# A chunked attention with a Fourier mix and an MLP: last weighting beside the next batch's first scores, and normed tiles made sooner

## The chip, the cores and the metric

The kernel runs on one core of a Trainium2 chip. The metric is device time in microseconds, the median of several runs. A profile is one more execution, recorded by the hardware; its span runs from its first to its last instruction, and its own device time is somewhat longer than its span.

## The reference

For 8 batches, 8 heads, 576 positions and 64 values a head: attention within chunks of 64 positions, then a two-dimensional Fourier transform whose real part is added to the attention's output, then a normalisation and a two-layer MLP, all in fp32.

```python
scores = scale * q_c @ k_c.T            # per chunk of 64
attn = softmax(scores)                  # minus the row maximum, exp, over the row sum
x = attn @ v_c                          # (B, S, H*D) = (8, 576, 512)
u = x + real(fft(fft(x, axis=1), axis=2))
un = (u - mean(u)) / sqrt(var(u) + 1e-6)
out = u + maximum(un @ w_ch1, 0) @ w_ch2     # 512 -> 2048 -> 512
```

## The kernel before

**Tiles and groups.** A tile is 128 positions of a batch (two chunks). A batch has four: two "lo" tiles from its start and two "hi" tiles from its end, read backwards, since the transform is folded about the middle. The ninth chunks of two batches share a "rest" tile, so even batches count five tiles and odd ones four. The MLP works on nine groups of four tiles: one for each batch, and a last one with the four rest tiles.

**The MLP** runs group after group and is the main line of the program. Groups 0 (both layers) and 1 (first layer) are plain: `up_first`, `up_plain`, `down_plain`. After that each layer is a scheme with seven products of half-size blocks in place of eight: `up_halves` (L997) for the first layer, in four pairs of row blocks, and `down_halves` (L1042) for the second. Both count o = 0 to 6 for the product and r = 0, 1 for the half that it serves. Each product goes to a half of a PSUM tile, `pa` (o = 0, 1, 4) or `pb` (o = 2, 3, 5, 6), and is evicted before the next one is needed: in `up_halves` o = 0 and o = 4 by ScalarE (L1019, L1029), the others by VectorE (L1021, L1023, L1025, L1031, L1034), with ScalarE's Relu after them. `operands` (L916 to L920) makes sums of the layer's results on VectorE and GpSimd.

**The attention and transform of the next batch** are generators of small steps (`side`, `attention`, `fourier`) that the last loop of the program (L1188 on) mixes into the MLP: after each `yield` of the MLP it takes as many steps as are due by a linear rule. So a batch's attention falls partly into a down phase and partly into the next up phase, and its transform into the down phase after that. For each tile `att_T` turns q and k (VectorE, and an extra column by GpSimd for lo tiles, L350), `att_S` makes the scores (16 matmuls of 64x64, L380), `softmax` takes the maximum and subtracts it on VectorE (L393, L395), `exponential` is ScalarE's, `att_P` transposes, and `att_V` weights v (16 matmuls of 64x65, L428) and divides on VectorE (L441 to L445). Within a batch the scores of tile n + 1 stand right behind the weighting of tile n. The first scores of a batch are a step of their own (L583, L584), which comes due in a down phase. After hi tiles `fold` (L487) makes sums and differences on GpSimd.

**From transform to MLP.** `fourier` ends with `mixed`, `both`, `added` and `means` (L686 to L720): for each pair of tiles a matmul group, VectorE's and GpSimd's additions, VectorE's statistics (L632, L633) and ScalarE's rstd (L636, L637). Then `normed` (L806) makes a normalised tile `un` on VectorE (L824), and `turned` (L827) transposes it on TensorE (L329) and copies it to `unT`, by ScalarE for even tiles and by VectorE for odd ones (L837, L835). `combined` (L839) forms differences of the turned tiles. `down_halves` calls these for the next group between its own products; it counts k = 2*o + r.

**PSUM buffers.** `ps_t`, two buffers, serves transposes, the mix, two of the transform's products and the weighting, which takes both. `ps_a`, one buffer, serves the scores and the transform's other products. `ps_f`, four buffers, is the MLP's.

**The start.** The first batch's attention and transform run ahead of everything (`attention_early`, `fourier_early`). `keep_warm` (L1139) issues matmuls on zeros into a spare tile, so that TensorE has something to do in the gaps.

Each engine works through its own instructions in the order of the program text as executed; waits are semaphores.

Of the kernel before, what the change touches and what calls it, by code (L numbers as in the profile page):

```python
# [16 lines left out]
def kernel(  # L17
# [33 lines left out]
    B, H, S, D = q.shape  # L51
# [321 lines left out]
    def att_S(n):  # L373
        a, b = qT.pop(n), kT.pop(n)
        sc = ps_a.tile([128, 2, 512], FP32, tag="att", name="sc")
        for j in range(NJ):
            for e in range(2):
                for c in range(2):
                    r0, t0 = e * D, c * CH
                    nc.tensor.matmul(  # L380
                        out=sc[t0:t0 + CH, e, j * CH:(j + 1) * CH],
                        lhsT=a[r0:r0 + D, 2 * j + c, 0:CH],
                        rhs=b[r0:r0 + D, 2 * j + c, 0:CH],
                        start=True,
                        stop=True,
                    )
        scs[n] = sc
# [139 lines left out]
    def attention_early():  # L527

        lo, hi = first[0], first[1] - 1

        def ready(n):
            if n == at[LO, 0, 1]:
                shift_early(0)
            if n == at[HI, 0, 1]:
                fold(0, 1)
            if n == at[HI, 0, 0]:
                fold(0, 0)
            if n + 3 > hi:
                load_v(n + 3)

        att_T(lo)
        att_S(lo)
        for n in range(lo, hi + 1):
            if n < hi:
                att_T(n + 1)
            softmax(n)
            if n > lo:
                att_V(n - 1)
                ready(n - 1)
            if n < hi:  # L550
                att_S(n + 1)
            if n in (lo, hi):
                keep_warm(1)
            att_P(n)
        shift_early(1)
        fold(0, NM)
        keep_warm(1)
        att_V(hi)
        ready(hi)
        keep_warm(3)  # L560
        turn_tables()
        round_next()
        round_next(put_off)

    def attention(b):

        lo, hi = first[b], first[b + 1] - 1

        def ready(n):

            if n == at[LO, b, NM - 1]:
                shift(b)
            for i in range(NM):
                if n == at[HI, b, i]:
                    fold(b, i)
            if n == at[HI, b, 0]:
                fold(b, NM)
            return kind(n) == HI

        if b > 1:  # L580


            att_S(lo)  # L583
            softmax(lo)  # L584
            yield
            for n in range(lo, hi + 1):
                exponential(n)
                if n + 1 < NT:
                    att_T(n + 1, "q")
                yield  # L590
                att_P(n)
                if n + 1 < NT:
                    att_T(n + 1, "k")
                yield
                att_V(n)
                if n < hi:
                    att_S(n + 1)
                    softmax(n + 1)
                if n + 3 < NT:
                    load_v(n + 3)  # L600
                yield ready(n)
            return
        att_T(lo)
        yield
        for n in range(lo, hi + 1):
            att_S(n)
            softmax(n)
            yield
            if n + 1 < NT:
                att_T(n + 1)  # L610
            yield
            if n > lo:
                att_V(n - 1)
                if n + 2 < NT:
                    load_v(n + 2)
                yield ready(n - 1)
            att_P(n)
            yield
        att_V(hi)
        if hi + 3 < NT:  # L620
            load_v(hi + 3)
        yield ready(hi)
# [204 lines left out]
    def turned(g, s):  # L827
        if s >= len(groups[g]):
            return
        if s == 0:  # L830
            unTs[g] = one_p.tile([128, KD, G * 128], FP32, tag="unT", name="unT")
        unT, un = unTs[g], uns.pop((g, s))
        pt = turn(lambda j: un[:, j * 128:(j + 1) * 128])
        if s % 2 and g > 1:
            nc.vector.tensor_copy(unT[:, :, s * 128:(s + 1) * 128], pt)  # L835
        else:
            nc.scalar.copy(unT[:, :, s * 128:(s + 1) * 128], pt)  # L837
# [204 lines left out]
    def down_halves(g, h1):  # L1042
        pas, pbs = {}, {}
        for o in range(NO):
            w = slab2[((g - first_of[2]) * NO + o) % NS2]
            for r in range(2):
                cl, ch = slice(r * 128, (r + 1) * 128), slice(256 + r * 128, 256 + (r + 1) * 128)
                low, high = groups[g][r], groups[g][2 + r]
                olow, ohigh = os_[:, 2 * r], os_[:, 2 * r + 1]
                a, b = tmp[:, r, 0], tmp[:, r, 1]  # L1050
                if o == 0:
                    pas[r] = ps_f.tile([128, 2, 256], FP32, tag="ff", name="pa")
                if o == 2:
                    pbs[r] = ps_f.tile([128, 2, 256], FP32, tag="ff", name="pb")
                dst = (pas, pas, pbs, pbs, pas, pbs, pbs)[o][r][:, (0, 1, 0, 1, 0, 0, 1)[o]]
                lhs = (
                    h1[:, 0:HF, cl], ys[:, :, cl], xs[:, :, cl], h1[:, 0:HF, ch],
                    h1[:, HF:KF, cl], ys[:, :, cl], h1[:, HF:KF, ch],
                )[o]
                for m in range(HF):  # L1060
                    nc.tensor.matmul(  # L1061
                        out=dst, lhsT=lhs[:, m], rhs=w[:, m],
                        start=(o in (0, 2) and m == 0), stop=(m == HF - 1), skip_group_check=True,
                    )
                if o == 0:
                    nc.scalar.copy(a, dst)
                elif o == 1:
                    nc.vector.tensor_tensor(out=b, in0=dst, in1=a, op=ALU.add)
                elif o == 2:
                    nc.vector.tensor_tensor(out=a, in0=dst, in1=b, op=ALU.add)  # L1070
                elif o == 3:
                    nc.vector.tensor_tensor(out=ohigh[:, HM:DM], in0=dst, in1=ohigh[:, HM:DM], op=ALU.add)
                    nc.gpsimd.tensor_tensor(out=olow[:, HM:DM], in0=b, in1=natural(low)[:, HM:DM], op=ALU.add)
                    nc.gpsimd.tensor_tensor(out=ohigh[:, 0:HM], in0=b, in1=natural(high)[:, 0:HM], op=ALU.add)
                elif o == 4:
                    nc.vector.tensor_tensor(out=olow[:, 0:HM], in0=dst, in1=natural(low)[:, 0:HM], op=ALU.add)
                elif o == 5:
                    nc.vector.tensor_tensor(out=olow[:, HM:DM], in0=dst, in1=olow[:, HM:DM], op=ALU.add)
                    store(low, olow)
                else:  # L1080
                    nc.vector.tensor_tensor(out=ohigh[:, 0:HM], in0=dst, in1=ohigh[:, 0:HM], op=ALU.add)  # L1081
                    store(high, ohigh)
                k = 2 * o + r
                if g + 1 < NG:
                    for j in range(G):
                        if k == 4 + 2 * j:
                            normed(g + 1, j)
                        if k == 5 + 2 * j:
                            turned(g + 1, j)
                            if j >= 2:  # L1090
                                combined(g + 1, j - 2)
                if r == 1:
                    if o == 1:
                        for j in range(0, HF, 2):
                            two = ys[:, j:j + 2]
                            nc.gpsimd.tensor_tensor(
                                out=two, in0=h1[:, HF + j:HF + j + 2, lo], in1=two, op=ALU.subtract
                            )
                    if o == 2:
                        for i in range(2):  # L1100
                            nc.gpsimd.tensor_tensor(
                                out=os_[:, 2 * i + 1, HM:DM], in0=tmp[:, i, 0],
                                in1=natural(groups[g][2 + i])[:, HM:DM], op=ALU.add,
                            )
                    fetch(2)
                yield
# [7 lines left out]
    with tc.manual_schedule():  # L1114
# [24 lines left out]
        def keep_warm(times):  # L1139

            for _ in range(times):
                nc.tensor.matmul(out=idle[:, 0:NQ], lhsT=warm[:, 0:128], rhs=warm[:, 0:NQ], start=True, stop=True)
# [130 lines left out]
```

## Time and profile before

| | |
|---|---|
| runs | 1107.84, 1108.06, 1110.43 us; median 1108.06 |
| profiled execution | 1109.99 us, span 1108.2 us |
| TensorE matmul | 1079.4 us busy, 97% of the span |
| VectorE, ScalarE, GpSimd | 53%, 27%, 25% |
| DMA | 192.73 MB, mean 174 GB/s |
| granted TensorE clock, mean | 0.998 |

Each row of a timeline gives start, length, engine, line, operation, what it writes from what, sizes and count, and in brackets the engine's idle time before it with what ended it. Most matmuls leave two records, and the records of a back-to-back row overlap, so distances are best taken from start to start. A list of waits gives total, number and longest. A row of stretches gives the busy time of each engine with its instructions, then the clock granted to TensorE in parts of full speed, and the DMA's share and rate.

### The profile page before, as it was taken

How to read it: one execution, taken by the hardware profiler on the slowest of the kernel's cores; microseconds unless marked ns; L12 is line 12 of the kernel's file. 1: busy time of each engine (PE TensorE's matmuls, PEld its weight loads, DVE VectorE, ACT ScalarE, POOL GpSimd, SP SyncE). 2: the span in 40 equal slices, each digit the busy share in tenths (PEclk: the TensorE clock that was granted, in tenths of full speed). 3: DMA queues.
4: the chain of work that ended last, by engine and by line, in shares of the span. 5: the costliest groups of instructions: out<-in, count | busy, mean ns of one | idle time of the engine just before them, and what ended most of it. 6: DMA issues, size and time to landing. Idle time of an engine off the chain costs nothing. (4 is left out here: it accounts for less than half of the span.)

```text
span 1108.2 us, 18749 instructions
## 1 busy us (share of the span) xinstructions
PE 1079.4 (97%) x7010; PEld 849.1 (77%) x7010; DVE 582.1 (53%) x1260; ACT 297.5 (27%) x725; POOL 277.4 (25%) x403
## 2 busy tenths in 40 slices
PE   8899999999999999999999999999999999999998
PEld 6644454447887888888888888788888888888887
DVE  4798987325566365663556455625554434323521
ACT  4588453212112311322022212221133102201210
POOL 4200102354405140244024220424042401120130
PEclk9999999999999999999999999999999999999999
DMA  7767656679566546683559357753653355446232
GB/s 169 227 178 193 154 169 229 177 245 287 182 188 191 162 141 199 197 249 108 168 170 251 115 167 211 202 178 132 202 168 111 114 183 178 134 152 200 85 114 76
DMA packets 147970, 192.73 MB, mean 174 GB/s; under 512 B 66126, under 2 KB 104014, under 8 KB 140712
## 3 DMA queue, kind: packets, MB, share of 16 engines
q1 hardware_dynamic: 145620, 190.20, 56.8%
q8 instruction: 56, 0.92, 0.3%
q0 software_dynamic: 512, 0.68, 0.3%
q10 hardware_dynamic: 1748, 0.66, 0.2%
q14 instruction: 34, 0.28, 0.1%
HBM read 167.22 MB, written 24.12 MB: 173 GB/s over the span
## 5 line engine op out<-in xcount | busy, mean ns | idle before, releaser
L920 POOL TENSOR_TENSOR h<-h 128x256 f32<-128x256 f32 x64 | 56.0, 880 | 269.0 <-PE pb L1014 153.1
L1061 PE MATMUL pa<-wb,h 128*128 128x256 f32 x512 | 114.4, 380 | 0.0
L1061 PE MATMUL pb<-wb,h 128*128 128x256 f32 x512 | 114.2, 380 | 0.0
L1014 PE MATMUL pb<-unT,wa 128*128 128x256 f32 x448 | 107.0, 382 | 3.7 <-DVE wa L1023 3.4
L1014 PE MATMUL pb<-wa 128*128 128x256 f32 x448 | 107.2, 382 | 2.6 <-DVE h L1031 2.6
L1061 PEld LDWEIGHTS pa<-wb,h 128*128 128x128 f32 x512 | 96.4, 190 | 13.4 <-issue 0.5
L1014 PE MATMUL pa<-unT,wa 128*128 128x256 f32 x448 | 106.6, 381 | 0.0
L1061 PEld LDWEIGHTS pb<-wb,h 128*128 128x128 f32 x512 | 96.1, 190 | 12.6
L1014 PEld LDWEIGHTS pb<-unT,wa 128*128 128x128 f32 x448 | 84.1, 190 | 19.0 <-DVE wa L1023 8.0
L1014 PEld LDWEIGHTS pb<-wa 128*128 128x128 f32 x448 | 83.8, 190 | 15.4 <-DVE h L1031 3.8
L1014 PEld LDWEIGHTS pa<-unT,wa 128*128 128x128 f32 x448 | 83.9, 190 | 11.1
L930 PE MATMUL up<-unT,wa 128*128 128x512 f32 x128 | 58.0, 600 | 2.0 <-ACT h L938 1.2
L968 PE MATMUL dn<-wb,h 128*128 128x512 f32 x128 | 57.4, 597 | 1.3 <-ACT h L938 1.3
L1061 PE MATMUL pa<-wb,yall 128*128 128x256 f32 x256 | 57.9, 381 | 0.0
L1061 PE MATMUL pb<-wb,yall 128*128 128x256 f32 x256 | 57.1, 381 | 0.0
L947 PE MATMUL up<-unT,wa 128*128 128x512 f32 x128 | 56.8, 596 | 0.0
L1029 ACT ACTIVATE h<-pa 128x256 f32<-128x256 f32 x56 | 21.5, 383 | 131.3 <-PE pa L1014 131.3
L1061 PE MATMUL pb<-wb 128*128 128x256 f32 x256 | 56.6, 379 | 0.0
L1021 DVE TENSOR_TENSOR wa<-pa,wa 128x256 f32<-128x256 f32 x56 | 23.8, 424 | 61.3 <-PE pa L1014 59.6
L1014 PE MATMUL pa<-wa 128*128 128x256 f32 x224 | 53.2, 380 | 0.7 <-ACT wa L1019 0.7
L1061 PEld LDWEIGHTS pb<-wb,yall 128*128 128x128 f32 x256 | 48.1, 190 | 6.5
L1061 PEld LDWEIGHTS pb<-wb 128*128 128x128 f32 x256 | 48.2, 190 | 6.2
(242 smaller groups left out, 1655.7 us busy)
## 6 DMA issues: line engine op xcount, KB each, us to landing
wb<-s SPq DMA_DIRECT2D x56, 1024.0 KB
wa<-s SPq DMA_DIRECT2D x196, 256.0 KB
xall<-in_moe_w_ch_dram SPq DMA_DIRECT2D x22, 512.0 KB
q<-in_q_dram SPq DMA_DIRECT2D x96, 112.0 KB
k<-in_k_dram SPq DMA_DIRECT2D x96, 112.0 KB
v<-in_v_dram SPq DMA_DIRECT2D x124, 64.0 KB
yall<-in_moe_w_ch_dram SPq DMA_DIRECT2D x10, 512.0 KB
s<-wb SPq DMA_DIRECT2D x20, 256.0 KB
```

The source lines that it names most:

```text
L920: nc.gpsimd.tensor_tensor(out=h1[:, m, hi], in0=h1[:, m, lo], in1=h1[:, m, hi], op=ALU.subtract)
L930: nc.tensor.matmul(out=up, lhsT=w1[:, kk, m * 128:(m + 1) * 128], rhs=unT[:, kk], start=(kk == 0), stop=(kk == KD - 1),)
L947: nc.tensor.matmul(out=up, lhsT=w1[:, kk, m * 128:(m + 1) * 128], rhs=unT[:, kk], start=(kk == 0), stop=(kk == KD - 1),)
L968: nc.tensor.matmul(out=dn, lhsT=h1[:, m, s * 128:(s + 1) * 128], rhs=w2[:, m, :], start=(m == 0), stop=(m == KF - 1),)
L1014: nc.tensor.matmul(out=dst, lhsT=w[:, kk, r], rhs=rhs[o][:, kk], start=(o in (0, 2) and kk == 0), stop=(kk == 1), skip_group_check=True,)
L1021: nc.vector.tensor_tensor(out=b, in0=dst, in1=a, op=ALU.add)
L1029: nc.scalar.activation(out=h1[:, m, lo], in_=dst, func=ACTF.Relu)
L1061: nc.tensor.matmul(out=dst, lhsT=lhs[:, m], rhs=w[:, m], start=(o in (0, 2) and m == 0), stop=(m == HF - 1), skip_group_check=True,)
```

## The change

1. In `attention_early` the last `keep_warm` issues six matmuls instead of three.
2. In `attention`, for batches 4 to 7, the first scores and their softmax are no longer a step of their own; they are issued right behind the last weighting of the batch before, that is of batches 3 to 6.
3. In `down_halves` `normed` for tile j is called at the end of k = 3 + 2j instead of 4 + 2j, and `turned` in the middle of the matmuls of k = 5 + 2j, ahead of that group's last four matmuls and of its eviction, instead of after the eviction. `combined` stays at the end of k = 5 + 2j.

The instructions of SyncE, ScalarE and GpSimd keep their order; those of TensorE and VectorE change places as described, and six records of idle matmuls come in.

```diff
@@ -557,7 +557,7 @@
         keep_warm(1)
         att_V(hi)
         ready(hi)
-        keep_warm(3)
+        keep_warm(6)
         turn_tables()
@@ -580,8 +580,9 @@
         if b > 1:
-            att_S(lo)
-            softmax(lo)
+            if b <= 3:
+                att_S(lo)
+                softmax(lo)
             yield
@@ -593,7 +594,7 @@
                 yield
                 att_V(n)
-                if n < hi:
+                if n < hi or 2 < b < B - 1:
                     att_S(n + 1)
                     softmax(n + 1)
@@ -1057,7 +1058,10 @@
+                k = 2 * o + r
                 for m in range(HF):
+                    if m == HF // 2 and g + 1 < NG and k in range(5, 5 + 2 * G, 2):
+                        turned(g + 1, (k - 5) // 2)
                     nc.tensor.matmul(
@@ -1080,15 +1084,12 @@
-                k = 2 * o + r
                 if g + 1 < NG:
                     for j in range(G):
-                        if k == 4 + 2 * j:
+                        if k == 3 + 2 * j:
                             normed(g + 1, j)
-                        if k == 5 + 2 * j:
-                            turned(g + 1, j)
-                            if j >= 2:
-                                combined(g + 1, j - 2)
+                        if k == 5 + 2 * j and j >= 2:
+                            combined(g + 1, j - 2)
```

## The prediction

> **What bounds the kernel now.** I read the page first: section 1 says which engine is full, section 4, the chain that ended last, names TensorE alone above 0% (20%; the rest of the span it does not place).
>
> ```profile
> PE 1079.4 (97%) x7010; PEld 849.1 (77%) x7010; DVE 582.1 (53%) x1260; ACT 297.5 (27%) x725; POOL 277.4 (25%) x403
> ```
>
> So time moves only where TensorE waits, restarts[...] or runs at a lower clock. Next came the view of who waited for whom, TensorE alone, for what the change can touch:
>
> ```profile
> PE pb L1014 <- DVE wa L1023: 3.4, 6, 0.9
> PE pb L1014 <- DVE h L1031: 2.6, 3, 1.3
> PE xp L428 <- ACT unT L837: 2.5, 6, 0.4
> PE z L740 <- POOL pm_rest L522: 2.4, 1, 2.4
> PE pt L329 <- DVE un L824: 2.1, 7, 0.4
> ```
>
> Columns: total, times, longest. The last three are the waits that the change aims at; the first two it may lengthen. Then the stretches around the 2.4 us wait: PEclk, the third figure from the right, is the granted clock.
>
> ```profile
> 29.70:33.10 3.40, 1.03 (x5) 0.87 (x5) 3.30 (x8) 2.12 (x6) 2.87 (x6) 1.00 0.80 211
> 33.10:36.50 3.40, 3.40 (x15) 1.92 (x14) 0.45 (x2) 1.97 (x3) 2.08 (x8) 0.50 0.96 377
> ```
>
> After a stretch with 1.03 us of work TensorE got half its clock for 3.4 us. Last, the timeline of TensorE in one down phase (halves) with the VectorE rows that answer to it, and in two up phases:
>
> ```profile
> 515.87 7.07 PE L1061 MATMUL pb<-wb 128*128 128x256 f32 x32
> 523.26 0.63 PE L329 MATMUL pt<-ident,un 128*128 128x128 f32 x4 [0.32 <-DVE un L824]
> ...
> 540.51 0.62 PE L428 MATMUL xp<-v,pT 64*64 64x65 f32 x26 [0.41 <-ACT unT L837]
> ```
> ```profile
> 521.44 0.69 DVE L632 BATCH_NORM_STATS2 bst<-xall 128x6 f32<-128x512 f32 x1 [1.45 <-POOL xall L712]
> ...
> 522.58 0.54 DVE L824 TENSOR_SCALAR un<-xall,st,rstd 128x512 f32<-128x512 f32 x1
> ```
> ```profile
> 573.75 0.70 PE L428 MATMUL xp<-v,pT 64*64 64x65 f32 x32
> 574.26 0.65 PE L380 MATMUL sc<-kT,qT 64*64 64x64 f32 x32
> 574.84 1.99 PE L1014 MATMUL pb<-wa 128*128 128x256 f32 x8
> 577.49 1.99 PE L1014 MATMUL pb<-unT,wa 128*128 128x256 f32 x8 [0.65 <-DVE wa L1023]
> ...
> 590.12 0.70 PE L428 MATMUL xp<-v,pT 64*64 64x65 f32 x32
> 590.75 1.99 PE L1014 MATMUL pb<-wa 128*128 128x256 f32 x8
> 592.58 1.95 PE L1014 MATMUL pb<-unT,wa 128*128 128x256 f32 x8
> ```
>
> I use starts, since a row's length holds the modelled tail. Unhindered, 8 records of 256 columns (four matmuls) take 1.73 us from start to start. A weighting (L428) with scores (L380) behind it is followed by a wait of 0.65 us for VectorE; a last weighting, with no scores, is not.
>
> [...] Here the block at 515.87 takes 7.39 us to the next start instead of 6.91, 0.48 for a wait of 0.32: 0.16 for the restart. [...] A `pb` tile is two halves, so a product into the second half waits until the first has been read; the wait at 577.49 fits that.
>
> **The change part by part.**
>
> *Three more idle matmuls* (L560). The six records at 27.97 space out at about 0.24 us (1.73 us with tail), so six more add 1.46 and end near 31.2. The product at 32.07 cannot start before ScalarE's last table copy (L253, 31.61 + 0.35 = 31.96), so the cover is the 2.37 us gap; without it they would cost 1.46. The idle rest is 0.9 us. Between 9.17 and 12.58 TensorE was busy for 2.34 us of 3.41 and kept its clock, so I take it that it keeps it here. Worth 3.4 x (1 - 0.50) = 1.70 us against this execution, which took 1109.99 (span 1108.2). The runs are 1107.84, 1108.06 and 1110.43: I guess that the first two did not have the half clock. Against the median: nothing, bounds 0 and -1.70.
>
> *Normed and turned sooner* (down_halves). No instruction is added; ScalarE, GpSimd and SyncE keep their order, and no transfer moves. VectorE's first `un` now stands behind the eviction of k = 3 (L1068, ends 516.07), ahead of the statistics that stall until 521.44 for GpSimd. Its rstd is done at 516.33, so it ends near 516.9. The four transposes now stand in the middle of group k = 5, four matmuls or 1.73 us sooner, near 521.4: 4 us to spare. Queued behind the normed tile on VectorE is L705 of the next mix, which started at 516.84 anyway. The 0.32 and 0.16 vanish: over the six batches the waits are 0.33, 0.22, 0.32, 0.23, 0.32, 0.27 = 1.69, restarts 6 x 0.16 = 0.96, sum 2.65. The third transposes move before the last four matmuls of k = 9, so ScalarE's copy (0.58 us, it started at 539.88) is done about a microsecond before the weighting wants its buffer. Weighting and scores took 539.77 to 541.59 = 1.82 there; the unhindered pair at 319.09 ends at 320.18 = 1.09. Five such places (the sixth is in a plain down phase and stays): 5 x 0.73 = 3.65. Transposes inside a group cost their 0.44 as now: at 531.45 four stand between two groups with nothing lost. What comes late next is VectorE's eviction of k = 4 (L1070, still held by the statistics, done at 522.66), half a microsecond before k = 6 wants its bank. Sum -6.30, bounds -3.75 (bare waits, 1.69 + 5 x 0.41) and -6.30.
>
> *Scores moved to the last weighting* (batches 3 to 6, four times). In the down phase scores cost 0.62 (523.82 to 524.44), 0.10 in the group behind, and 0.09 in the transposes ahead (0.56 against 0.47 at 878.65, where no scores follow): 0.81. At the new place VectorE, behind the weighting's 1.2 us (L441, L442, L445), must first do the maximum and the subtraction (0.68 + 0.69), and the evictions L1023 or L1034 are queued behind them; TensorE waits for their bank. Priced by pairs. Batches 3 and 5 have it behind o = 1: V to the end of the second product, 573.75 to 579.32 = 5.57 with scores, 590.12 to 594.37 = 4.25 without: 1.32; in the other phase 5.57 against 4.34: 1.23. Batches 4 and 6 have it behind o = 5: 701.82 to 708.82 = 7.00 against 717.39 to 723.30 = 5.91: 1.09. Net +0.42 +0.51 +0.28 +0.28 = +1.5. q and k of the next tile are turned in time (VectorE's kT at 588.66 ends 1.0 us before the scores would start; GpSimd's extra column at 712.19, five before). Bounds: no wait at all, 1.09 - 0.63 = 0.46 against 0.81, four times: -1.4; the second wait too, which the present pairs have a product later (1.34 and 0.86, with restart 1.50 and 1.02): +1.5 + 2 x 1.50 + 2 x 1.02 = +6.5. I take +1.5, as that second wait has a q transpose (L348, 1.1 us) in VectorE's queue, and none follows a last weighting.
>
> Sum: -6.3 + 1.5 = -4.8, and -1.7 in an execution like the profiled one: 1109.99 - 6.5 = 1103.5; from the median, 1108.06 - 4.8 = 1103.3. I say **1103.4**.
>
> **Rivals.** (1) *Scores find the gap empty*: GpSimd's folding, not the softmax, makes VectorE late, and the bank wait is hidden. -4.8 - 2.9 = 1100.4. For it: at 320.18 and 557.57 pairs have no wait; against: those stand ahead of o = 0, which ScalarE evicts. (2) *VectorE becomes the bound at the moved scores*: the second wait comes as well; 1103.4 + 5.0 = 1108.4, no change. For it: L918 and L919 take 0.6 to 1.0 us each while GpSimd folds, and their 3.6 us between the evictions just fill TensorE's 3.5. Against: no q transpose there. Half of it gives 1105.9. (3) *Slower, the normed tile is late*: transposes are asked for 1.73 us sooner. Were `un` still held by the statistics (ready 523.1), TensorE would wait 2.05 + 0.16 = 2.2 each, six times 13.2, in place of 2.65; 1108.06 + 13.2 - 2.65 - 3.65 + 1.5 = 1116.5. It decides once `un` ends after 521.4. Against it: the written order puts it ahead of them. (4) *The idle matmuls do nothing*: in the sum already, for the median.
>
> **How the numbers follow.** The likeliest case 0.60, its own range 1102.3 to 1104.7. Rival 1, whole or in part, 0.13; rival 2 or part of it 0.21; rival 3 or something like it 0.06. From 1101.2 to 1106.2 lie the likeliest, half of rival 1, and half of rival 2. About 0.3%, 3.3 us, is what a measurement can tell from no change: the likeliest case and rival 1 lie below 1104.7 (0.72 with the edge taken off), rival 2 and the edge within (0.21), rival 3 and the far end of 2 partly above (0.07).
>
> **What would show it.** TensorE's list: the wait of `pt` for `un` falls from 2.1 to about 0.4 (an early one stays), `xp` for `unT` from 2.5 to 0.4, `z` for the folding to 0.9 with PEclk 1.00 after it; `pb` for L1023 rises by some 1.3 and `pa` for ScalarE's L1019 by 0.7. Wrong if L1031 rises by more than 1 us (rival 2), or if `pt` still waits in the down phases (rival 3).

## The result, and the profile after

The changed kernel takes 1102.86 us (median of six runs, 1101.77 to 1104.80), the kernel before 1109.33 in six runs of the same comparison: a ratio of 0.9944 [0.9930, 0.9958], or 6.5 us less. A later repeat gave 0.9943 [0.9929, 0.9958]. The profiled execution takes 1102.55 us with a span of 1100.74, against 1109.99 and 1108.17 before: 7.44 less, where the prediction had 6.5 for that execution.

The page's row of engines comes first. TensorE was busy for 1079.4 us and is now busy for 1076.5; its share has hardly moved, for it is still the only engine near its full span.

```profile
PE 1076.5 (98%) x7016; PEld 847.0 (77%) x7016; DVE 583.0 (53%) x1260; ACT 296.3 (27%) x725; POOL 280.2 (25%) x403
```

The list of TensorE's waits in the changed kernel (total, times, longest). Lines of the up phases stand one further down than before: L1015, L1020, L1024 and L1032 were L1014, L1019, L1023 and L1031.

```profile
PE pb L1015 <- DVE wa L1024: 4.8, 8, 0.7
PE pb L1015 <- DVE h L1032: 2.4, 3, 1.1
...
PE pa L1015 <- ACT wa L1020: 1.5, 4, 0.4
...
PE z L741 <- POOL pm_rest L522: 0.6, 1, 0.6
PE sc L380 <- DVE rd L441: 0.6, 1, 0.6
PE pt L329 <- DVE un L825: 0.4, 1, 0.4
PE xp L428 <- ACT unT L838: 0.4, 1, 0.4
```

The three waits that the change aims at fell from 2.1, 2.5 and 2.4 us to 0.4, 0.4 and 0.6. VectorE's eviction of `pb` (now L1024) rose from 3.4 to 4.8, and its list has two more places. L1032, where a second wait would have shown, is at 2.4 instead of 2.6.

Stretches around the early gap (length, then busy time of PE, PEld, DVE, ACT and POOL with their instructions, granted clock, DMA share, GB/s):

```profile
29.70:33.10 3.40, 2.75 (x12) 1.87 (x11) 3.20 (x9) 2.12 (x6) 3.11 (x7) 1.00 0.85 249
33.10:36.50 3.40, 3.40 (x22) 2.33 (x21) 1.00 (x5) 1.97 (x3) 2.20 (x8) 1.00 1.03 413
```

The first stretch now has 2.75 us of TensorE work instead of 1.03, and the second runs at full clock (1.00) instead of half (0.50).

The timeline of TensorE in the same down phase as before the change, then the VectorE rows that answer to it (start, length, engine, line, operation, tiles; in brackets the idle time ahead and what ended it):

```profile
513.27 5.35 PE L1065 MATMUL pb<-wb 128*128 128x256 f32 x24
518.46 0.60 PE L329 MATMUL pt<-ident,un 128*128 128x128 f32 x4
518.89 1.89 PE L1065 MATMUL pb<-wb 128*128 128x256 f32 x8
...
534.02 1.89 PE L1065 MATMUL pa<-wb,h 128*128 128x256 f32 x8
535.85 0.70 PE L428 MATMUL xp<-v,pT 64*64 64x65 f32 x32
536.36 0.65 PE L380 MATMUL sc<-kT,qT 64*64 64x64 f32 x32
```
```profile
513.78 1.20 DVE L825 TENSOR_SCALAR un<-xall,st,rstd 128x512 f32<-128x512 f32 x1 [0.29 <-ACT rstd L638]
...
519.05 0.69 DVE L633 BATCH_NORM_STATS2 bst<-xall 128x6 f32<-128x512 f32 x1 [1.45 <-POOL xall L713]
...
519.88 0.39 DVE L1074 TENSOR_TENSOR wa<-pb,wa 128x256 f32<-128x256 f32 x1
```

The transposes (518.46) stand between two parts of one product and wait for nothing. `un` ends at 514.98, 3.5 us ahead of them; the statistics that it used to stand behind now stand behind it, and still stall 1.45 us for GpSimd. The weighting at 535.85 starts without the 0.41 us that it had. The eviction that comes late next (L1074) ends at 520.27; k = 6 begins at 520.62.

Last, one of the four moved scores in its up phase, on TensorE and on VectorE:

```profile
585.25 0.70 PE L428 MATMUL xp<-v,pT 64*64 64x65 f32 x32
585.77 0.65 PE L380 MATMUL sc<-kT,qT 64*64 64x64 f32 x32
586.34 1.99 PE L1015 MATMUL pb<-wa 128*128 128x256 f32 x8
588.99 1.99 PE L1015 MATMUL pb<-unT,wa 128*128 128x256 f32 x8 [0.65 <-DVE wa L1024]
590.82 1.89 PE L1015 MATMUL pa<-unT,wa 128*128 128x256 f32 x8
```
```profile
587.20 0.68 DVE L393 TENSOR_REDUCE mx<-sc 128x8 f32<-128x512 f32 x1
587.91 0.69 DVE L395 TENSOR_TENSOR ex<-sc,mx 128x512 f32<-128x512 f32 x1
588.52 0.74 DVE L1024 TENSOR_TENSOR wa<-pb,wa 128x256 f32<-128x256 f32 x2
```

The same 0.65 us that the pair at 573.75 had before. From the weighting to the end of the second product it is 590.82 - 585.25 = 5.57 us, the number that the prediction took from that pair.

**Where the 7.4 us went.** The table cuts the span at the first product of each MLP phase and gives the length of each kind of phase, less that of the kernel before. The columns after the first are experiments described below.

| us against before | changed | moved scores alone | sooner alone | idle matmuls and sooner |
|---|---|---|---|---|
| up to the first MLP product | -1.32 | -0.77 | +0.87 | -0.83 |
| up phase of group 1 (plain) | -1.02 | -0.36 | -0.68 | -0.71 |
| six down phases (halves) | -9.76 | -3.28 | -6.46 | -6.47 |
| five up phases (halves) | +4.67 | +6.61 | -0.08 | -0.93 |

The down phases add up: -3.28 - 6.46 = -9.74, where the whole has -9.76. Single up phases differ by up to 0.8 us also where no edit touches them, which is dealt with under the first experiment.

### The profile page after: what moved, and what is told of

Its sections match the earlier page's. It is cut to its first block, busy times and chain, and to the rows that moved or that the text cites. A ratio compares the mean times of both kernels' runs of the same rounds, so it can differ in the third digit from the quotient of the medians.

```text
span 1100.7 us, 18766 instructions
## 1 busy us (share of the span) xinstructions
PE 1076.5 (98%) x7016; PEld 847.0 (77%) x7016; DVE 583.0 (53%) x1260; ACT 296.3 (27%) x725; POOL 280.2 (25%) x403
## 4 chain that ended last, share of the span: by engine, by line
PE 83%; DVE 6%; DMA 5%; ACT 3%; SPq 1%; issue 1%; POOL 1%; DVEq 0%; ACTq 0%; POOLq 0%
PE pb L1065 19%; PE pa L1065 15%; PE pb L1015 14%; PE pa L1015 11%; PE dn L969 5%; PE up L948 4%; PE pt L329 3%; PE up L931 2%; PE more_z L648 2%; DMA q<-in_q_dram 2%; PE mix L696 2%; PE z L648 2%; PE xp L428 1%; PE sc L380 1%; DMA k<-in_k_dram 1%
## 5 line engine op out<-in xcount | busy, mean ns | idle before, releaser
L1015 PE MATMUL pb<-unT,wa 128*128 128x256 f32 x448 | 107.0, 382 | 5.1 <-DVE wa L1024 4.8
L1015 PE MATMUL pb<-wa 128*128 128x256 f32 x448 | 107.2, 382 | 2.4 <-DVE h L1032 2.4
L1015 PE MATMUL pa<-unT,wa 128*128 128x256 f32 x448 | 106.6, 381 | 0.0
L1015 PEld LDWEIGHTS pb<-unT,wa 128*128 128x128 f32 x448 | 84.0, 190 | 20.8 <-DVE wa L1024 9.7
L1015 PEld LDWEIGHTS pb<-wa 128*128 128x128 f32 x448 | 83.7, 190 | 15.3 <-DVE h L1032 3.6
L1015 PEld LDWEIGHTS pa<-unT,wa 128*128 128x128 f32 x448 | 83.8, 190 | 11.2
L1015 PE MATMUL pa<-wa 128*128 128x256 f32 x224 | 53.4, 381 | 1.5 <-ACT wa L1020 1.5
L1065 PEld LDWEIGHTS pa<-wb,yall 128*128 128x128 f32 x256 | 47.7, 190 | 6.4
```

The source lines that it names most:

```text
L1015: nc.tensor.matmul(out=dst, lhsT=w[:, kk, r], rhs=rhs[o][:, kk], start=(o in (0, 2) and kk == 0), stop=(kk == 1), skip_group_check=True,)
L1065: nc.tensor.matmul(out=dst, lhsT=lhs[:, m], rhs=w[:, m], start=(o in (0, 2) and m == 0), stop=(m == HF - 1), skip_group_check=True,)
```

## The experiments

**Each part alone.** Four kernels, measured side by side, each put together from hunks of the change: the moved scores alone, `normed` and `turned` sooner alone, the idle matmuls alone, and the last two together (the change without the moved scores).

```diff
 # moved scores alone
-            att_S(lo)
-            softmax(lo)
+            if b <= 3:
+                att_S(lo)
+                softmax(lo)
...
-                if n < hi:
+                if n < hi or 2 < b < B - 1:
```
```diff
 # sooner alone
+                    if m == HF // 2 and g + 1 < NG and k in range(5, 5 + 2 * G, 2):
+                        turned(g + 1, (k - 5) // 2)
...
-                        if k == 4 + 2 * j:
+                        if k == 3 + 2 * j:
                             normed(g + 1, j)
-                        if k == 5 + 2 * j:
-                            turned(g + 1, j)
...
```
```diff
 # idle matmuls alone
-        keep_warm(3)
+        keep_warm(6)
```

> Before with the moved first scores alone. My theory (VectorE's maximum and subtraction stand ahead of the evictions that TensorE's next bank needs): slower by 1.5 us than before; TensorE's wait for L1023 rises from 3.4 to about 4.7 us, for ScalarE's L1019 from 0.7 to about 1.4, L1031 stays at 2.6 within 0.3. Rival (the wait is hidden[...]): faster by 1.4 us, no wait rises. Rival (VectorE becomes the bound): slower by 3 to 6.5 us, L1031 rises by more than 1 us.

> Before with the sooner normed and turned tiles alone. My theory: faster by 6.3 us; TensorE's wait of pt for un falls from 2.1 to 0.4 and of xp for unT from 2.5 to 0.4, and the blocks behind them lose their restart. Rival (only the bare waits come back, or they turn into others): faster by 3.8 us or less, with a new wait in the down phases.

> Before with six idle matmuls in place of three. My theory: the span is 1.7 us below an execution of before with a half clock behind the early gap and equal to one without; over many runs 0 to 1.7 us faster. The profile shows PEclk 1.00 behind the gap. Rival (the idle matmuls delay the first transform product): slower by up to 1.5 us, with no wait left ahead of it.

> The change without the moved scores. My theory: 1.5 us faster than the changed kernel, 6.3 to 8.0 us faster than before; waits for L1023 at 3.4 us and for L1019 at 0.7 us as before, those of pt for un and xp for unT at 0.4. Rival (the moved scores pay once the transposes have left the down phase): 1 us or more slower than the changed kernel.

| | median us | ratio to before (1109.55) | in us |
|---|---|---|---|
| moved scores alone | 1111.64 | 1.0017 [1.0008, 1.0026] | +1.9 |
| sooner alone | 1102.98 | 0.9935 [0.9915, 0.9955] | -7.2 |
| idle matmuls alone | 1108.15 | 0.9990 [0.9981, 0.9998] | -1.1 |
| idle matmuls and sooner | 1101.29 | 0.9926 [0.9909, 0.9944] | -8.2 |

The three parts sum to -6.4, against -6.2 for the whole by its ratio. So the change is one part that gains and two that are small, one of them a loss: without the moved scores the kernel has the lower ratio, by 0.0018, though the two intervals overlap.

The waits of TensorE with the moved scores left out (these three lines have the numbers of the kernel before):

```profile
PE pb L1014 <- DVE wa L1023: 2.5, 5, 0.7
...
PE pa L1014 <- ACT wa L1019: 0.7, 2, 0.4
```

With them, in the changed kernel, it is 4.8 in eight places and 1.5 in four. With the moved scores alone (lines as in the changed kernel):

```profile
PE pb L1015 <- DVE wa L1024: 6.3, 8, 1.8
PE pb L1015 <- DVE h L1032: 2.8, 3, 1.5
...
PE pa L1015 <- ACT wa L1020: 1.5, 4, 0.4
```

The longest of these waits, in TensorE's timeline of that run, and the VectorE row that explains it:

```profile
713.49 1.99 PE L1015 MATMUL pb<-unT,wa 128*128 128x256 f32 x8 [1.75 <-DVE wa L1024]
```
```profile
712.07 1.10 DVE L348 STREAM_TRANSPOSE qT<-q 128x512 f32<-128x512 f32 x1 [1.55 <-DMA q<-in_q_dram]
```

VectorE stood 1.55 us in front of a transpose of q whose transfer had not landed, with the eviction queued behind it. TensorE's wait at this place was 0.86 before, 0.38 in the changed kernel and 1.75 here, each time 0.2 us more than VectorE's wait for q (0.66, 0.17, 1.55), and no edit changes SyncE's order. Such waits differ from one execution to the next, as these three do. With what they changed taken out, the moved scores cost 1.33, 1.09, 1.33 and 1.10 us in the changed kernel: 4.85, where the prediction had 4.73.

**The two halves of "sooner", one at a time.** `turned` alone goes into the middle of its group with `normed` left at k = 4 + 2j; then `normed` alone at k = 3 + 2j with `turned` where it was.

```diff
 # turned alone
...
+                    if m == HF // 2 and g + 1 < NG and k in range(5, 5 + 2 * G, 2):
+                        turned(g + 1, (k - 5) // 2)
...
-                        if k == 5 + 2 * j:
-                            turned(g + 1, j)
-                            if j >= 2:
-                                combined(g + 1, j - 2)
+                        if k == 5 + 2 * j and j >= 2:
+                            combined(g + 1, j - 2)
```
```diff
 # normed alone
-                        if k == 4 + 2 * j:
+                        if k == 3 + 2 * j:
                             normed(g + 1, j)
```

> Before with turned in the middle of k = 5 + 2j, and normed left at the end of k = 4 + 2j. My theory: the first normed tile of a group is then still behind the statistics that wait for GpSimd, and TensorE asks for it 1.73 us sooner; six waits of pt for un of about 2.1 us in place of six of 0.3, 12 to 13 us in all, while the five waits of xp for unT go: 11 - 3.7, about 7 us slower than before. Rival (the normed tile does not depend on its place): no longer wait than before, 3.7 us faster.

> Before with normed at the end of k = 3 + 2j, and turned left behind the group. My theory: the waits of pt for un go (2.1 to 0.4 us) with their restarts, those of xp for unT stay at 2.5: 2.6 us faster than before. Rival (the two edits gain only together): no change.

`turned` alone takes 1118.74 us, 1.0079 [1.0059, 1.0100], +8.8. Its wait list, and one of the six places on TensorE's timeline:

```profile
PE pt L329 <- DVE un L824: 12.4, 7, 2.1
```
```profile
526.35 0.63 PE L329 MATMUL pt<-ident,un 128*128 128x128 f32 x4 [2.04 <-DVE un L824]
```

This is the rival of the late normed tile, in the flesh: six waits of 1.94 to 2.05 us, for the 2.05 that it named. The sum by that rival's terms is 13.2 - 2.65 - 3.65 = 6.9; the run is two microseconds dearer, and in the profiled execution the stretches around that wait show one reason:

```profile
523.97:527.38 3.41, 1.36 (x9) 1.01 (x8) 1.64 (x4) 0.86 (x3) 1.42 (x2) 1.00 0.00 0
527.38:530.79 3.41, 3.41 (x39) 2.37 (x37) 0.42 (x1) 0.22 (x1) 0.38 (x1) 0.50 0.02 5
```

The stretch with this wait (2.04 us) had 1.36 us of work, and the next 3.41 us ran at half clock (0.50): by estimate 3.41 x 0.50 = 1.7 us more. The other five waits were not followed by half clock (the mean of the execution is 0.997).

`normed` alone takes 1106.88 us, 0.9976 [0.9965, 0.9987], -2.7, which is the 2.65 of the first transposes. Its waits:

```profile
PE xp L428 <- ACT unT L837: 2.5, 6, 0.4
...
PE pt L329 <- DVE un L824: 0.4, 1, 0.4
```

The wait for `un` is gone, and the weighting's wait for ScalarE's copy has stayed. So the earlier `normed` is worth 2.7, and the earlier `turned` loses 8.8 without it and gains with it. How much it gains is best read from the six down phases of the profiles: 2.84 us less with `normed` alone and 6.46 with both, so 3.62, where the prediction had 3.65. The medians give 4.5 (7.2 - 2.7), but the interval of the 7.2 alone is 2.2 us wide on either side.

**The softmax held back.** If the price of the moved scores is the maximum and the subtraction in front of an eviction, then leaving the scores where they are and issuing only these two later should take it away. In the changed kernel `att_S` stays behind the last weighting, and its `softmax` waits in a list until the evictions of o = 6 have been issued.

```diff
                     att_S(n + 1)
-                    softmax(n + 1)
+                    if n < hi:
+                        softmax(n + 1)
+                    else:
+                        held.append(n + 1)
...
                         nc.scalar.activation(out=h1[:, HF + m], in_=h1[:, HF + m], func=ACTF.Relu)
+                        if r == 1 and held:
+                            softmax(held.pop())
```

> The changed kernel with the maximum and subtraction of the moved scores (four times) held until after the evictions of o = 6, where ScalarE has the next one. My theory (the softmax in VectorE's queue makes the waits, not the scores): the four waits of 0.74, 0.65 (L1024) and twice 0.37 (L1020) go with about 0.7 us of restarts, 2.8 us faster than the changed kernel and 1.3 us faster than the change without the moved scores, 1100.0 us. Rival (the weighting's own division, or GpSimd's folding, makes VectorE late): the waits stay within 0.2 us each, no gain over the changed kernel.

It takes 1100.39 us, 0.9913 [0.9899, 0.9928]. Measured again, beside the changed kernel:

> The kernel with the held softmax once more, beside the changed kernel on the same chip. My theory: 2 to 3 us below the changed kernel. Rival (the gain seen was a matter of when q and k land): within 1 us of it.

> The changed kernel itself, for the comparison with the held softmax on the same chip. Both theories: 6 to 7 us below before.

1099.57 us, 0.9914 [0.9899, 0.9928], against 1102.67, 0.9943 [0.9929, 0.9958]: 3.1 us below the changed kernel. Its waits (L1028 and L1024 are L1024 and L1020 of the changed kernel, which had 4.8 us in eight places and 1.5 in four):

```profile
PE pb L1019 <- DVE wa L1028: 3.1, 5, 0.8
...
PE pa L1019 <- ACT wa L1024: 0.7, 2, 0.4
```

The same place on TensorE and VectorE:

```profile
584.11 0.70 PE L428 MATMUL xp<-v,pT 64*64 64x65 f32 x32
584.62 0.65 PE L380 MATMUL sc<-kT,qT 64*64 64x64 f32 x32
585.20 1.99 PE L1019 MATMUL pb<-wa 128*128 128x256 f32 x8
587.03 1.89 PE L1019 MATMUL pb<-unT,wa 128*128 128x256 f32 x8
588.75 1.89 PE L1019 MATMUL pa<-unT,wa 128*128 128x256 f32 x8
```
```profile
586.36 0.42 DVE L1028 TENSOR_TENSOR wa<-pb,wa 128x256 f32<-128x256 f32 x1 [0.23 <-PE pb L1019]
...
594.48 0.68 DVE L393 TENSOR_REDUCE mx<-sc 128x8 f32<-128x512 f32 x1
```

VectorE now waits for the product, not the product for VectorE; the maximum comes 8 us later, and no new wait of TensorE shows. From the weighting to the end of the second product it is 588.75 - 584.11 = 4.64 us, not 5.57. The down phases keep their whole gain (-9.75 against before), and the up phases cost +1.32 instead of +4.67. So the wait came from the softmax on VectorE, and not from the scores on TensorE. Whether the moved scores pay once their softmax is held is not shown: the kernel without them has 0.9926 [0.9909, 0.9944], and the intervals overlap.

**Every softmax held.** The same for all scores in up phases: each `softmax` waits until the evictions of o = 2 or o = 6, when its scores fall behind o = 1 or o = 5.

```diff
                     att_S(n + 1)
-                    softmax(n + 1)
+                    held.append(n + 1)
+                    if where[0] not in (1, 5):
+                        release()
...
+                if o in (2, 6):
+                    release()
                 fetch(1)
                 if o in (1, 3, 5, 6):
+                    where[0] = o
                     yield h1
```

> The changed kernel with every softmax of an up phase that stands behind o = 1 or o = 5 held: behind the evictions of o = 2 or of o = 6. My theory: besides the gain of holding the moved ones (2.8 us) the seven waits of batches 3 to 7 shrink by some 3 us, half of them left over where a q transpose and the folding fill VectorE (L1032): 1097 us. Rival (VectorE is full there, and a wait taken away at o = 3 comes back at o = 6): L1032's waits rise from 2.4 to 4 us or more, and the gain is that of holding the moved ones alone, 1100 us.

1103.07 us, 0.9929 [0.9916, 0.9942]: slower than either expectation, and some 1.8 us above holding only the four by the ratios. Their intervals overlap, but the up phases of the two profiles say the same: +3.00 us against before, not +1.32. In the waits (L1041 and L1033 are L1032 and L1024 of the changed kernel), and at one place of TensorE's timeline:

```profile
PE pb L1024 <- DVE h L1041: 5.6, 5, 1.9
...
PE pb L1024 <- DVE wa L1033: 2.9, 3, 1.6
```
```profile
343.61 1.99 PE L1024 MATMUL pb<-wa 128*128 128x256 f32 x8 [1.94 <-DVE h L1041]
```

One wait fell by 1.9 us and the next eviction's rose by 3.2; at this place waits of 0.65 and 1.10 became one of 1.94. VectorE had room behind the evictions of o = 6 that follow a last weighting, and none behind those of o = 2.

**None and nine of the idle matmuls.** On the changed kernel, the six become zero, then nine.

```diff
-        keep_warm(6)
+        keep_warm(0)     # and, in the other kernel, keep_warm(9)
```

> The changed kernel with none of the six idle matmuls ahead of the first transform product. My theory: TensorE's gap there grows from 0.65 to about 3.7 us, the clock falls to half for 3.4 us behind it in most executions, and the kernel is 0 to 1.7 us slower than the changed one, in the profile 1.7 if the half clock shows. Rival (the clock does not follow the gap): no change, PEclk 1.00.

> The changed kernel with nine idle matmuls in place of six. My theory: they last 0.73 us longer than the gap has left (0.65), so the wait of the first transform product goes and it starts some 0.1 us late or not at all: no change within 0.3 us, the clock stays full. Rival (the gap that is left still lowers the clock in some executions): up to 1 us faster than the changed kernel.

None: 1105.46 us, 0.9962 [0.9947, 0.9977], some 2 us above six by the ratios, though the intervals overlap. The mean granted clock of its six runs is 0.995 to 0.998; with six idle matmuls it is 0.999 or 1.000. Nine: 1102.63 us, 0.9935 [0.9922, 0.9948], no different from six. The stretches without them:

```profile
30.45:33.86 3.41, 0.81 (x2) 0.70 (x3) 2.73 (x7) 2.12 (x6) 2.51 (x5) 0.50 0.90 240
33.86:37.27 3.41, 3.41 (x16) 1.92 (x14) 0.76 (x2) 1.97 (x3) 0.82 (x3) 0.50 1.02 397
```

The gap is 4.6 us; the stretch in which it ends and the next one ran at half clock (0.50), 6.8 us in all. With nine the product's wait is gone from the list. On TensorE's timeline of that run the product (`z`) now starts at 32.46, 0.54 us after the end of ScalarE's last table copy (L253, 31.92); with six it was 0.10 us after it (32.31 and 32.21). So nine overfill the gap by some 0.4 us, too little to be seen in the ratio:

```profile
27.98 4.65 PE L1143 MATMUL idle<-warm 128*128 128x289 f32 x18
...
32.46 1.14 PE L741 MATMUL z<-tk,pm 128*128 128x289 f32 x4
```

## Why the prediction was right, step by step

**The sum.** 1103.4 was said and 1102.86 measured. That this came so near is in part luck: as a fall from the median 4.7 us were said and 6.5 measured, and the median of three runs that the prediction started from, 1108.06, lay 1.3 below the 1109.33 of six. In the profiled execution 6.5 were said and 7.44 measured; there the parts come out within 0.4 us each, and what is left is a phase that the prediction did not count (below).

**Normed and turned sooner: right, -6.30 said, -6.46 measured** in the six down phases, both in the kernel with this part alone and in the one with the idle matmuls as well. Five phases gave 1.13 to 1.24 and the last 0.47, as it should, for no weighting stands in it. The step "VectorE's first `un` ends near 516.9, 4 us to spare" was off in one term: `un` took 1.20 us instead of 0.54 (more on this in the last section), and 3.5 us were left. It cost nothing.

**Moved scores: right in mechanism and nearly in size, +1.5 said.** Removed from the down phases: 4 x 0.81 = 3.24 said, 3.28 measured in the run with this part alone. Added to the up phases: 4.73 said, 4.85 measured. Net +1.6, and +1.9 as the ratio of that run. Pairs out of the trace before, with and without scores at the same place, had held the whole cost, restart and queue included. That TensorE waits for the eviction is in the traces: 0.65 us at 588.99 until VectorE's L1024, and no wait in the run with the held softmax, where the eviction (586.36) comes ahead of the next product (587.03). Why a product into one half of a `pb` tile waits until the other half is evicted was not shown.

**Idle matmuls: the mechanism was right, two terms were mis-sized.** The wait came to 0.65 us instead of 0.9, as the idle matmuls began 0.51 us later than before (28.48) and ScalarE's last table copy ended only 0.25 later (32.21). The half clock is gone (1.00 where it was 0.50), but the start gained 1.32 us and not 1.70: the first scores began at 9.72 us here and at 9.22 before, which the edit does not touch. The step "against the median: nothing" failed. It took the three runs at hand for runs without the half clock. In the later comparison of 43 runs of the kernel before, 24 had a mean granted clock of 0.999 or more and a median of 1108.8 us, 19 had 0.998 or less and 1111.2 (one stretch of half clock as long as the one before, 3.4 us, takes 3.4/1108 x 0.5 = 0.0015 off the mean). The mean does not say where such a stretch lay, but with the idle matmuls alone 20 of 22 runs had 0.999 or more. So the median of before is that of a mixture, 1109.3 to 1109.6, and the three runs had caught its lower side; the part is worth 1.1 us of it.

**Not foreseen: the up phase of group 1**, 1.02 us shorter. Its wait for the scores' buffer (`sc` for L441) fell from 1.65 to 0.63. It does not follow the edits: of the other twelve traces eleven have this phase 0.36 to 1.22 us shorter than before and one (`normed` alone) 0.32 longer. So it is put down to variation between executions. The scores wait for the weighting's division, which stands on VectorE behind a transpose of k (L348), and that transpose waits for k to land: it began 36.10 us into the phase before and 35.06 now, and the scores 1.14 and 1.16 us after it. Why k lands sooner in one execution than in another was not found.

**The rivals.** *Scores find the gap empty* fell: VectorE's wait rose by the 1.4 us that the likeliest case named (1.3). *VectorE becomes the bound* fell: L1032 is at 2.4, and at 2.8 with the moved scores alone. When every softmax was held, VectorE did become the bound, at o = 6, with 5.6. *The normed tile is late* fell for this change, and was shown to be what `turned` alone does. *The idle matmuls do nothing* fell, for the median too.

## What to carry to other kernels

A product moved to another place on a full engine is best priced by two places in the trace that differ only in having it, from start to start; here that was right to 0.1 us a place, while the matmuls' own time would have made a gain of 1.4 us out of the moved scores, which lose 1.5 to 2. Before a consumer is asked for sooner, look where its producer stands in its own engine's queue: the same move of the transposes loses 8.8 us or gains 3.6, depending on whether the normed tile stands ahead of a stall or behind it. What hurt the full engine here was not the step that was moved but what it issues on another engine's queue in front of an eviction; that part could be held back alone (3.1 us less), so long as the place to which it was held had room.

## What the runs showed of the hardware that was not expected

**Half clock behind stretches that were far from idle.** In these traces half clock (0.50) followed stretches of 3.4 us with 1.03 (the kernel before), 1.36 (`turned` alone) and, in the run without idle matmuls, 1.24 us of TensorE work:

```profile
579.99:583.40 3.41, 1.24 (x7) 0.76 (x6) 1.93 (x4) 0.74 (x2) 2.84 (x7) 1.00 0.79 236
583.40:586.82 3.42, 3.42 (x12) 2.75 (x11) 1.54 (x3) 1.29 (x3) 0.55 (x1) 0.50 0.74 216
```

In the run with the moved scores alone it stayed full (1.00) after the early gap: a stretch of 3.42 us there had 1.59 us of work (28.28 to 31.70), one of 3.40 us that lies over the same gap had 0.47 (29.40 to 32.80), and the clock was 1.00 in both and in those behind them. So neither the work in a stretch nor the length of the gap says alone whether half clock follows: the gap of 2.4 us before was followed by it, this one of 3.0 us was not. What decides it was not shown. One wait of 2.04 us for an operand, of the six of `turned` alone, came to cost 1.7 us more than itself, by the estimate in the experiment.

**A normed tile that takes twice as long.** L825 took 1.19 to 1.20 us in six places and 1.04 in a seventh, and 0.54 in the 24 others. In the seven GpSimd was already at an instruction of L1097 when `un` began, and in each `un` ended 0.28 to 0.29 us after that instruction did. The GpSimd row beside the `un` at 513.78:

```profile
512.19 5.59 POOL L1097 TENSOR_TENSOR yall<-h,yall 128x512 f32<-128x512 f32 x4
```

In seven other places an instruction of GpSimd's L1102 began 0.16 to 0.22 us after `un` had begun, and `un` kept its 0.54. So here `un` looks as if it had waited for the GpSimd instruction that it found running, and had not merely run slower beside it. No run of its own tests that.
